# Pairing the last four token blocks already in the first half of a two-pass MLP behind a retention attention

## The chip, the cores and the metric

The kernel runs on one core of one Trainium2 chip. The metric is the time of one execution on the device in microseconds (us). Five engines work side by side, each through its own queue of instructions in order: TensorE (PE, matrix products), VectorE (DVE), ScalarE (ACT), GpSimd (POOL) and SyncE (SP, which here issues every DMA).

## The reference, cut to what matters

```python
B, H, S, D = 8, 8, 576, 64                       # attention
scores = q @ k.T / sqrt(D)                       # for each batch and head
ret    = scores * Dmat                           # gamma**(i-j) for i >= j, else 0
x      = (ret @ v) -> (B*S, H*D) = (4608, 512)   # heads side by side
h      = x @ w_in                                # 512 -> 2048
g      = max(h, 0) + alpha * min(h, 0)
out    = g @ w_out                               # 2048 -> 512
```

All inputs and the output are float32.

## The kernel before, in words

**Attention.** Eight batches times four pairs of heads make 32 joints, the first eight (two batches) worked in parts at the start. Of a joint, `operands` scales and transposes q and k; `joint` computes the values of the joint before it (`values`, L851) and its own scores and chunk sums on PE (L903, L910, L913), masks the scores on DVE (L931), sums the chunks on ACT and DVE in `su` (L943 to L954), and DMAs `su` into `vn`, from where the next call's values read it. ACT copies the values into the block's x tile (`keep_x`, L870). Values go to the PSUM banks `psh`, scores and sums to `psa`. `todo` says after which cell a joint is called.

**The MLP.** 4608 tokens are 18 blocks of 256 (`kb`). 2048 hidden columns are eight units `u` of 256. Weights of four units fit in SBUF (`wsl`), so there are two halves: all blocks with units 0 to 3, then all with 4 to 7. What a block has summed in the first half goes to DRAM (`ok`) and comes back (`op`) in the second; a block's x goes to DRAM (`xk`) and back too. `order` lists the visits (a block and its units), and a cell is one unit of one visit.

Every float32 operand is written as three pieces of which a product takes three matmuls. `split_x` makes those of a block's x, `split_w` those of a weight matrix, `split_g` (L1204 to L1211, two steps on ACT and two on POOL) those of the activated hidden block `g`. Some of the DVE and POOL steps are chained by `lock=True`: one that follows on the other engine waits for the one before.

A cell's first layer is `unit` for one block: 24 matmuls of 256 columns (L1151), 12 for each half of the unit's hidden columns, and for each half ACT, DVE, ACT, DVE (L1158 to L1165) into `ga`. `unit_two` does it for two blocks at once: 2 x 12 matmuls of 512 columns (L1181), the halves in `psh` and `psa`, the same four steps at twice the width (L1187 to L1193). The second layer, `second`, is 12 matmuls of 512 columns for a cell (L1232) into four banks `pso`; after a visit's last cell `evacuate` (L1250 to L1255) writes the sum out.

Before the change the first half is 17 blocks one by one and then block 17 with all eight units in one visit; the second half is 16 blocks in 8 pairs, and the last one single. Pairs may use `psa` since attention has ended by then (its last call stands after cell 56; the first 68 cells are the first half). In pairs, x pieces lie in turn in the room that unit 3's weights leave and in the two rooms `lxs` (`two_rooms`). The weights of unit 4 lie in twelve `planes`, the tiles that attention has left (`kx`, `qx`, `kn`, `kT`, `qT`, `at`, `su`, `wa`); those of units 5 to 7 take the rooms of units 0 to 2. Their 16 matrices come back from DRAM and are split while single blocks still run (`late`).

**What sets the order.** All steps are recorded with a cost, then `plan` puts them in an order engine by engine, by due times worked out backwards; PE may take any of the next 150 recorded steps. On the chip each engine follows that order strictly. `LAG` and `PUMP` say how many second layers stay behind the first ones. 

## Time and profile before

| | us |
|---|---|
| median of 3 runs | 931.44 |
| lowest and highest | 930.61, 931.87 |
| profiled execution, its own time | 930.41 |
| its span in the profile | 928.7 |

Busy time of the engines in the profiled execution: PE 918.4 us, weight loads 779.4, DVE 532.5, ACT 552.6, POOL 579.3. The costliest groups of PE are L1232 (second layer), L1151 (first layer of single blocks) and L1181 (of pairs). The matmuls are pipelined, so that the mean duration of one (392 ns with 512 columns, 284 with 256) is longer than the time from one to the next; what a group takes of PE's time is read from the chain of work. A few per cent of the matmuls have no record in the trace, so the counts that matter are taken from the built order of instructions.

### The profile page before, as it was taken

The page shows a single profiled execution, that of the slowest core. Times are in us where ns is not written, and L with a number is a line of the kernel's source. Part 1 is how long each engine was busy: PE and PEld are TensorE (multiplying, and loading weights), DVE is VectorE, ACT ScalarE, POOL GpSimd, SP SyncE. Part 2 cuts the span into 40 slices and gives each one's busy share as a digit, 9 for nine tenths or more (in the row PEclk, how much of TensorE's full clock was granted, in tenths as well). Part 3 has the DMA queues.
Part 4 walks back from the last instruction along what each step waited for, and adds up shares of the span by engine and source line. Part 5 has one row for each costly group of instructions (what it writes and reads, how often), then busy time and mean ns, then how long its engine had stood idle before and what let it go on. Part 6 is the DMA issues. An engine that isn't in the chain of part 4 may idle for free.

```text
span 928.7 us, 20968 instructions
## 1 busy us (share of the span) xinstructions
PE 918.4 (99%) x8101; PEld 779.4 (84%) x8101; DVE 532.5 (57%) x1070; ACT 552.6 (60%) x1178; POOL 579.3 (62%) x491
## 2 busy tenths in 40 slices
PE   8999999999999999999999999999999999999998
PEld 7676798988888898988999988888888888888887
DVE  7677666667666667766755764443454444434333
ACT  4566557566666667666876885554546363635342
POOL 5676867558765677655666465837465655647363
PEclk9999999999999999999999999999999999999999
DMA  9997587798887859864444421121212222221112
GB/s 231 241 233 144 127 203 151 176 206 175 195 199 193 193 138 221 191 150 130 148 137 147 126 80 68 47 91 46 91 54 82 68 86 95 70 68 46 46 46 68
DMA packets 235524, 120.93 MB, mean 130 GB/s; under 512 B 203408, under 2 KB 203424, under 8 KB 235424
## 3 DMA queue, kind: packets, MB, share of 16 engines
q1 hardware_dynamic: 235424, 119.59, 50.9%
q8 instruction: 64, 1.05, 0.5%
q14 instruction: 36, 0.29, 0.1%
HBM read 74.19 MB, written 31.98 MB: 114 GB/s over the span
## 4 chain that ended last, share of the span: by engine, by line
PE 90%; DMA 3%; DVE 2%; POOL 2%; SPq 1%; issue 1%; ACT 1%; POOLq 0%; DVEq 0%; ACTq 0%
PE pso L1232 39%; PE psh L1151 22%; PE psh L1181 9%; PE psa L1181 9%; PE psh L851 3%; PE psa L913 2%; PE psh L1082 2%; PE pso L1113 1%; SPq L208 1%; POOL w L775 1%; DMA kn<-in_k_dram 1%; DMA w<-in_moe_w_in_dram 1%; PE psh L903 1%; PE psa L910 1%; DMA lx<-in_moe_w_in_dram 0%
## 5 line engine op out<-in xcount | busy, mean ns | idle before, releaser
L1232 PE MATMUL pso<-w,g 128*128 128x512 f32 x1416 | 347.1, 392 | 0.0
L1232 PEld LDWEIGHTS pso<-w,g 128*128 128x128 f32 x1416 | 259.6, 188 | 50.7
L1151 PEld LDWEIGHTS psh<-lx,w 128*128 128x128 f32 x1608 | 202.4, 191 | 8.4 <-ACT x L870 1.1
L1151 PE MATMUL psh<-lx,w 128*128 128x256 f32 x1608 | 208.5, 284 | 0.7 <-ACT x L870 0.5
L1211 POOL TENSOR_TENSOR g<-g 128x512 fp32r<-128x512 f32 x136 | 176.0, 1294 | 24.2 <-DVE w L1057 4.1
L1208 POOL TENSOR_TENSOR g<-ga,g 128x512 fp32r<-128x512 f32 x72 | 93.2, 1294 | 122.9 <-ACT g L1204 107.9
L1159 DVE SCALAR_TENSOR_TENSOR ga<-psh,ga 128x256 f32<-128x256 f32 x144 | 60.6, 421 | 70.6 <-ACT ga L1158 68.9
L1158 ACT COPY ga<-psh 128x256 f32<-128x256 f32 x144 | 53.5, 372 | 69.5 <-PE psh L1151 60.8
L1208 POOL TENSOR_TENSOR g<-x,g 128x512 fp32r<-128x512 f32 x40 | 51.7, 1295 | 63.5 <-ACT g L1204 61.0
L1165 DVE SCALAR_TENSOR_TENSOR ga<-psh,malpha,ga 128x256 f32<-128x256 f32 x144 | 68.6, 477 | 22.4 <-ACT psh L1162 21.4
L1061 POOL TENSOR_TENSOR lx<-lx 128x512 fp32r<-128x512 f32 x48 | 61.9, 1296 | 20.1 <-DVE lx L1057 13.1
L1162 ACT ACTIVATE psh<-ga 128x256 f32<-128x256 f32 x144 | 55.7, 387 | 30.4 <-DVE ga L1159 30.2
L1204 ACT ACTIVATE g<-ga 128x512 fp32r<-128x512 f32 x72 | 45.4, 631 | 22.3 <-DVE ga L1165 15.0
L1208 POOL TENSOR_TENSOR g<-vn,g 128x512 fp32r<-128x512 f32 x24 | 31.1, 1294 | 41.6 <-ACT g L1204 38.4
L931 DVE SCALAR_TENSOR_TENSOR at<-psa,pf,mask 64x512 f32<-64x512 f32 x48 | 36.0, 750 | 25.8 <-PE psa L910 24.9
L1206 ACT ACTIVATE g<-ga 128x512 fp32r<-128x512 f32 x72 | 44.7, 621 | 0.0
L1250 DVE TENSOR_TENSOR op<-pso,op 128x512 f32<-128x512 f32 x34 | 23.3, 686 | 36.8 <-PE pso L1232 36.7
L1204 ACT ACTIVATE g<-x 128x512 fp32r<-128x512 f32 x40 | 25.1, 630 | 32.1 <-PE pso L1232 17.1
L1188 DVE SCALAR_TENSOR_TENSOR x<-psh,x 128x512 f32<-128x512 f32 x20 | 13.8, 690 | 45.0 <-PE psh L1181 45.0
L851 PEld LDWEIGHTS psh<-at,vn 128*64 128x64 f32 x864 | 27.7, 137 | 10.8 <-issue 6.0
L1057 POOL TENSOR_TENSOR lx<-x,lx 128x512 fp32r<-128x512 f32 x24 | 31.1, 1295 | 8.7 <-ACT lx L1054 5.4
L1181 PE MATMUL psh<-lx,w 128*128 128x512 f32 x144 | 34.7, 389 | 0.0
(292 smaller groups left out, 1695.9 us busy)
## 6 DMA issues: line engine op xcount, KB each, us to landing
xk<-x SPq DMA_DIRECT2D x18, 512.0 KB, 4.1
out_dram<-o SPq DMA_DIRECT2D x36, 256.0 KB, 2.0
ok<-o SPq DMA_DIRECT2D x34, 256.0 KB, 3.2
x<-xk SPq DMA_DIRECT2D x17, 512.0 KB, 5.7
op<-ok SPq DMA_DIRECT2D x17, 512.0 KB, 4.0
qx<-in_q_dram SPq DMA_DIRECT2D x96, 72.0 KB, 3.4
kx<-in_k_dram SPq DMA_DIRECT2D x96, 72.0 KB, 3.1
kn<-in_k_dram SPq DMA_DIRECT2D x48, 144.0 KB, 3.7
```

The costliest lines, as they stand in the source:

```text
L851: nc.tensor.matmul(pv[i].get()[half(h2), (j - js[0]) * C:(j - js[0] + 1) * C], vns[n % 2][:, h2, j], mt.get()[:, h2, j], start=True, stop= ...
L1061: lambda l=l, d=d, h=view(0, c): nc.gpsimd.tensor_tensor(out=piece(d()), in0=h(), in1=l(), op=ALU.subtract),
L1151: nc.tensor.matmul(at(b), w[:, c0:c0 + P], xp(l, cc), start=(n == 0 and cc == 0), stop=(n > 0 and cc == NCC - 1), skip_group_check=True)
L1158: do("ACT", 0.36, lambda g=g, at=at: nc.scalar.copy(g(), at(1)), [(ph, 1)], [(ga, f)])
L1159: do("DVE", 0.42, lambda g=g, at=at: nc.vector.scalar_tensor_tensor(out=g(), in0=at(0), scalar=ONE, in1=g(), op0=ALU.mult, op1=ALU.subtrac ...
L1162: do("ACT", 0.39, lambda g=g, at=at: nc.scalar.activation(at(1), g(), ACTF.Relu, scale=-1.0), [(ga, f)], [(ph, 1)])
L1165: do("DVE", 0.48, lambda g=g, at=at, fc=fc: nc.vector.scalar_tensor_tensor(out=g(), in0=at(1), scalar=malpha[:, fc:fc + 1], in1=g(), op0=A ...
L1181: nc.tensor.matmul(p.get(), w[:, c0:c0 + P], piece(words_of(g)[:, o:o + DM]), start=(l != 1 and cc == 0), stop=(l > 0 and cc == NCC - 1))
L1204: do("ACT", 0.64, lambda: nc.scalar.mul(piece(to.get()[:, 2]), whole(), BELOW), both, [(to, 2)])
L1208: do("POOL", 1.29, lambda: nc.gpsimd.tensor_tensor(out=piece(to.get()[:, 1]), in0=whole(), in1=to.get()[:, 2], op=ALU.subtract), both + [( ...
L1211: do("POOL", 1.29, lambda: nc.gpsimd.tensor_tensor(out=piece(to.get()[:, 2]), in0=to.get()[:, 0], in1=to.get()[:, 1], op=ALU.subtract), [( ...
L1232: nc.tensor.matmul(a[2 * m + b].get(), piece(g.get()[:, l, f, m * P:(m + 1) * P]), w_piece(u, 2 + f, l), start=(cell["first"] and f == 0 a ...
```

## The change

- The order of visits. Blocks 0 to 15 with units 0 to 3, then blocks 16 and 17 with units 3, 0, 1, 2; then the second half, which begins with blocks 16 and 17 and goes on with 0 to 15.
- Blocks 0 to 13 of the first half stay single; blocks 14 and 15, and 16 and 17, make two pairs, and all 18 blocks of the second half make nine. The second half's first pair reads the x pieces that the first half's last pair has made.
- The x pieces of the first pair (14, 15) lie in the twelve planes; those of the second in `lxs`.
- The 16 late weight matrices are split in pairs 1 and 2 (counted from 0), their raw words in the `ga` tiles of single blocks, with the ACT, POOL and DVE steps that the first 16 matrices have always had; the form through PSUM goes, as does that of `split_x`.
- Attention is called after other cells: its last values after cell 53, in the visit of block 13.
- The 16 conversions of second-half weights begin at cell 8 instead of 10.

```diff
@@ tile_retnet_parallel__then__act_prelu_kernel
+    PAIRS_AT = [8, 10, 12, 14, 16, 18, 20, 22, 24, 26, 29, 31, 33, 35, 37, 39, 42, 44, 46, 48, 49, 50, 51, 53]
@@ split_w
         do("ACT", 0.64, lambda: nc.scalar.mul(h(), full(), BELOW), [key], [w[0]])
-        if raw:
-            hp = Gen(psa[at % 2])
-            do("ACT", 0.6, lambda: nc.scalar.mul(piece(hp.get()), full(), BELOW), [key], [(hp, 0)])
-            do("DVE", 0.69, lambda: nc.vector.tensor_tensor(
-                out=l(), in0=full(), in1=hp.get(), op=ALU.subtract), [key, (hp, 0)], [w[1]])
-            do("DVE", 0.69, lambda: nc.vector.scalar_tensor_tensor(
-                out=d(), in0=hp.get(), scalar=ONE, in1=full(), op0=ALU.mult,
-                op1=ALU.subtract), [key, (hp, 0)], [w[2]])
-            return
         do("POOL", 1.29, lambda: nc.gpsimd.tensor_tensor(
             out=l(), in0=full(), in1=hf(), op=ALU.subtract), [key, w[0]], [w[1]], lock=True)
         do("DVE", 0.7, lambda: nc.vector.scalar_tensor_tensor(
@@ order
-    order = [(kb, (0, 1, 2, 3)) for kb in range(NKB - 1)]
-    order += [(NKB - 1, range(NU))]
-    order += [(kb, (4, 5, 6, 7)) for kb in range(NKB - 1)]
+    order = [(kb, (0, 1, 2, 3)) for kb in range(NKB - 2)]
+    order += [(kb, (3, 0, 1, 2)) for kb in (NKB - 2, NKB - 1)]
+    order += [(kb, (4, 5, 6, 7)) for kb in (NKB - 2, NKB - 1, *range(NKB - 2))]
@@ two_rooms
     def two_rooms(n):
-        if n % 2:
+        if n == 0:
+            rooms_of = ((g, i * DM) for g, i in planes())
+            return {(l, cc): next(rooms_of) for l in range(3) for cc in range(NCC)}, DM
+        if n == 1 or n % 2 == 0:
             gg = [Gen(x) for x in lxs]
             return {(l, cc): (gg[cc // 2], (l * 2 + cc % 2) * DM)
                     for l in range(3) for cc in range(NCC)}, DM
@@ split_x
-        late = vis["n"] >= LATE_X and rooms is None
...
-                if late:
-                    h = Gen(psa[n])
-                    ht = lambda h=h: h.get().rearrange("p (c t) -> p c t", t=TB)
-                    do("ACT", 0.6, lambda c=c, ht=ht: nc.scalar.mul(piece(ht()), raw(c), BELOW),
-                       keys, [(h, 0)])
-                    do("DVE", 0.7, lambda c=c, ht=ht, l=l: nc.vector.tensor_tensor(
-                        out=piece(l()), in0=raw(c), in1=ht(), op=ALU.subtract),
-                        keys + [(h, 0)], key(1, c))
-                else:
-                    do("ACT", 0.64 if wide else 0.38,
-                       lambda c=c, d=d: nc.scalar.mul(piece(d()), raw(c), BELOW), keys, key(2, c))
-                    eng, cost, tt = (("POOL", 1.29, nc.gpsimd) if rooms is None else
-                                     ("DVE", 0.69 if wide else 0.42, nc.vector))
-                    do(eng, cost, lambda c=c, l=l, d=d, tt=tt: tt.tensor_tensor(
-                        out=piece(l()), in0=raw(c), in1=d(), op=ALU.subtract),
-                        keys + key(2, c), key(1, c), lock=True)
+                do("ACT", 0.64 if wide else 0.38,
+                   lambda c=c, d=d: nc.scalar.mul(piece(d()), raw(c), BELOW), keys, key(2, c))
+                eng, cost, tt = (("POOL", 1.29, nc.gpsimd) if rooms is None else
+                                 ("DVE", 0.69 if wide else 0.42, nc.vector))
+                do(eng, cost, lambda c=c, l=l, d=d, tt=tt: tt.tensor_tensor(
+                    out=piece(l()), in0=raw(c), in1=d(), op=ALU.subtract),
+                    keys + key(2, c), key(1, c), lock=True)
@@ after the start
-    for i, at in enumerate((8, 10, 12, 14, 16, 18, 20, 22, 24, 26, 29, 31, 33, 35, 37, 39, 42, 44, 46, 48, 50, 52, 54, 56)):
+    for i, at in enumerate(PAIRS_AT):
...
-    turn = cells.index(next(c for c in cells if c["u"] == NS)) - NS
-    late = {turn - 8 + 2 * i: [16 + i] for i in range(4)}
-    for i in range(3):
-        for n in range(4):
-            late.setdefault(turn + 1 + i + n // 2 * LAG, []).append(20 + 4 * i + n)
...
-    ahead = {10 + 3 * i: 1 for i in range(16)}
+    ahead = {8 + 3 * i: 1 for i in range(16)}
@@ start_x, two
     def start_x(vis):
         kb = vis["kb"]
-        if "from" not in vis and (kb not in xb or NPAIR * (ready_kb[kb] + 1) in done):
+        if vis.get("two", (0,))[0] == 2:
+            at, step, side = visits[vis["n"] - 2]["x"]
+            vis["x"] = at, step, side
+        elif "from" not in vis and (kb not in xb or NPAIR * (ready_kb[kb] + 1) in done):
             fetch_x(vis)
-    turned_to = next(v["n"] for v in visits if 4 in v["us"])
-    two = [(visits[n], visits[n + 1]) for n in range(turned_to + 1, len(visits) - 1, 2)]
+    singles = NKB - 4
+    two = [(visits[n], visits[n + 1]) for n in range(singles, len(visits), 2)]
     for i, (va, vb) in enumerate(two):
         va["two"], vb["two"] = (i, 0), (i, 1)
-    visits[-1]["two"] = len(two), 0
@@ at_cell and after
-        for at in late.get(n, ()):
-            if at == 16:
-                planes_of.append(planes())
-            split_w(at, raw_room(), [next(planes_of[0]) for _ in range(3)] if at < 20 else None)
...
+    def split_first(at):
+        if not planes_of:
+            planes_of.append(planes())
+        split_w(at, Gen(gas[at % 2]), [next(planes_of[0]) for _ in range(3)])
...
     for cell in cells[8:]:
         vis = cell["vis"]
-        if vis["n"] > turned_to:
+        if vis["n"] == singles:
             break
         at_cell(cell)
         nxt = vis["n"] + 1
-        if vis["n"] < turned_to:
-            if cell["last"] or vis["n"] > 3:
-                start_x(visits[nxt])
-                if cell["last"]:
-                    next_x(visits[nxt])
-        elif cell["u"] in (NS + 1, NS + 2):
-            next_x(visits[nxt + cell["u"] - NS - 1])
-
-    ga_rooms = [xs[2], xs[3], xs[4]]
-    ga_kept = [raw_rooms[n] for n in range(2)]
-    nga = [0]
+        if nxt == singles:
+            if cell["u"] > 1:
+                next_x(visits[nxt + cell["u"] - 2])
+        elif cell["last"] or vis["n"] > 3:
+            start_x(visits[nxt])
+            if cell["last"]:
+                next_x(visits[nxt])
+
+    ga_rooms = [xs[3], xs[4], xs[2]]
+    nga = [3]
@@ pump
         for _ in range(k):
             if queue and "ga" in queue[0]:
                 ahead_g(1)
-                second(queue.pop(0))
+                c = queue.pop(0)
+                second(c)
+                if c["vis"]["n"] == singles + 3 and c["u"] < NS - 1:
+                    split_later(c["u"], 1)
                 ahead_g()
+
+
+    def split_later(u, half_of):
+        for n in range(2):
+            at = (NS + 1 + u) * 4 + 2 * half_of + n
+            split_w(at, Gen(gas[at % 2]))
@@ the loop over pairs
+            if i == 1:
+                if nu < 2:
+                    split_first(16 + 2 * nu)
+                    split_first(17 + 2 * nu)
+                if a["u"] < NS - 1:
+                    split_later(a["u"], 0)
             nxt = va["n"] + 2 + (nu - 1)
             if nu in (1, 2) and nxt < len(visits):
                 next_x(visits[nxt])
-    for cell in of[visits[-1]["n"]]:
-        unit(cell)
-        queue.append(cell)
-        pump(3)
-        ahead_g()
```

In the lines above `two_rooms` counts pairs from 0, `NS` is 4, `NKB` 18 and `NU` 8.

More of the change, by code (lines that the diff above doesn't have):

```diff
@@ L1260, in evacuate @@
             P * DM * 4, [(o, 0)], [(okm[kb], m)])
-    LATE_X = next(v["n"] for v in visits if 4 in v["us"]) - 3
     spare = Gen(lxs[1])
@@ L1401 @@
     todo = {}
-    for i, at in enumerate((8, 10, 12, 14, 16, 18, 20, 22, 24, 26, 29, 31, 33, 35, 37, 39, 42, 44, 46, 48, 50, 52, 54, 56)):
+    for i, at in enumerate(PAIRS_AT):
         todo.setdefault(at, []).append(2 * NPAIR + 1 + i)
     assert sum(map(len, todo.values())) == len(pairs) - 2 * NPAIR
-    turn = cells.index(next(c for c in cells if c["u"] == NS)) - NS
-    late = {turn - 8 + 2 * i: [16 + i] for i in range(4)}
-    for i in range(3):
-        for n in range(4):
-            late.setdefault(turn + 1 + i + n // 2 * LAG, []).append(20 + 4 * i + n)
-    raw_rooms = [Gen(None) for _ in range(2)]
-    ahead = {10 + 3 * i: 1 for i in range(16)}
-    nraw = [0]
-    def raw_room():
-        n = nraw[0] % 3
-        nraw[0] += 1
-        if n == 2:
-            return Gen(xs[3])
-        g = Gen(None)
-        was = raw_rooms[n] if raw_rooms[n].ops else vnm[n]
-        g.before, g.tile = list(was.ops), vns[n]
-        raw_rooms[n] = g
-        return g
+    of = {}
+    for cell in cells:
+        of.setdefault(cell["vis"]["n"], []).append(cell)
+    raw_rooms = [Gen(None) for _ in range(2)]
+    ahead = {8 + 3 * i: 1 for i in range(16)}
     def planes():
@@ L1477 @@
     planes_of = []
-    of = {}
-    for cell in cells:
-        of.setdefault(cell["vis"]["n"], []).append(cell)
+    def split_first(at):
+        if not planes_of:
+            planes_of.append(planes())
+        split_w(at, Gen(gas[at % 2]), [next(planes_of[0]) for _ in range(3)])
     for cell in cells[8:]:
         vis = cell["vis"]
-        if vis["n"] > turned_to:
+        if vis["n"] == singles:
             break
@@ L1504, in ga_room @@
         g = Gen(None)
-        g.before, g.tile = list(ga_kept[n - 3].ops), vns[n - 3]
-        ga_kept[n - 3] = g
+        g.before, g.tile = list(raw_rooms[n - 3].ops or vnm[n - 3].ops), vns[n - 3]
+        raw_rooms[n - 3] = g
         return g
```

## The prediction

> **What bounds the kernel.** I read the busy shares first, then who TensorE (PE) waits for, then the chain that ended last.
>
> ```profile
> span 928.7 us, 20968 instructions
> PE 918.4 (99%) x8101; PEld 779.4 (84%) x8101; DVE 532.5 (57%) x1070; ACT 552.6 (60%) x1178; POOL 579.3 (62%) x491
> PE 90%; DMA 3%; DVE 2%; POOL 2%; SPq 1%; issue 1%; ACT 1%; POOLq 0%; DVEq 0%; ACTq 0%
> ```
>
> PE is busy throughout and makes 90% of the chain. The view of stretches says where it is not:
>
> ```profile
> 0.00:60.00 60.00, 54.42 (x921) 40.53 (x921) 42.26 (x104) 31.27 (x53) 36.88 (x47) 1.00 1.00 241
> 60.00:440.00 380.00, 378.93 (x4764) 327.76 (x4766) 258.29 (x567) 244.73 (x580) 256.72 (x206) 1.00 0.78 176
> 440.00:548.00 108.00, 108.00 (x720) 98.36 (x715) 68.89 (x141) 83.93 (x188) 65.84 (x56) 1.00 0.43 137
> 548.00:888.00 340.00, 340.00 (x1499) 280.56 (x1498) 148.14 (x232) 178.22 (x329) 197.63 (x167) 1.00 0.20 66
> ```
>
> Columns: stretch, length, busy PE, weight loads, DVE, ACT, POOL, clock, DMA share, GB/s. PE is idle 5.6 us in the start, 1.1 us during attention (60 to 440), nothing after. So removed PE work comes off the end one for one, and each new PE wait goes on it one for one.
>
> The price of the two forms stands in the chain, single blocks first, then pairs (start, us, what, how many matmuls):
>
> ```profile
> 486.49 2.87 PE psh L1151 x24
> 489.37 2.75 PE pso L1232 x12
> ...
> 627.33 2.72 PE psh L1181 x12
> 630.05 2.72 PE pso L1232 x12
> 632.77 2.72 PE psa L1181 x12
> ```
>
> 24 matmuls of 256 columns take 2.87 us (119.6 ns each); 12 of 512 take 2.72 (226.7 ns), or 2.75 where 256-column ones follow.
>
> **What the Trainium skill says.** "Perfetto Trace Analysis", Identifying the Most-Contended Engine: matmul busy share is a bad measure of headroom, the weight-load share a better one. That is 84% here, so PE idles little but is not at its peak. "TensorE: Matmul & The Clock Gate", Back-to-back issue gap: an isolated gap of N/2.4 + 2.5 ns, as an estimate 109 and 216 ns; the trace has 120 and 227. The same section's sustained 131 ns at N = 512 does not hold in this trace. Doubling N thus saves little: 12.5 ns a pair. "SBUF — State Buffer", Two separate sides: DVE and GpSimd share a port pair under an exclusive lock. The trace agrees in kind: DVE waited 19.2 us in 7 waits for POOL before L1057.
>
> **The change, part by part.**
>
> 1. *Wider first matmuls.* The built instruction order has 1728 matmuls of L1151 before and 1152 after, 768 of L1181 before and 1056 after, L1232 1632 in both. Blocks 14 to 17 in the first half are 8 pair-units; in the second half two blocks that ran single become 4 more. Each of the 12 saves 2 x 2.87 - 2 x 2.72 = 0.30 us: 3.6 us. Their 24 second-layer batches go from 2.75 to 2.72: 0.7 us. **Sum: -4.3 us**, all on the path.
>
> 2. *Pieces and transfers.* Block 16 is split once, not twice, one x read of 512 KB goes, one output round trip (512 KB each way) comes with 2 + 2 DVE evacuation steps of 0.69 us. All lies beside PE, in stretches with DMA at 0.2 to 0.43 and DVE at 44 to 64%. I take 0; without that cover the late piece would be op, at L1250, and so the pso banks.
>
> 3. *Second-half weights.* 16 matrices are split during pairs 1 and 2. Each loses an ACT and a DVE step (0.60 and 0.68 us), and its L775 form (1.28 us, POOL) with L777 (0.69 us, DVE) replaces the PSUM form. A pair-unit lasts 10.88 us on PE; POOL's four steps of L1208 and L1211 fill 5.2. The 16 need 16 x (1.28 + 0.69) = 32 us of the shared lock, about 6 units of slack; they stand over some 7, and pair 2 splits no x. Two raw rooms of gas, each held for a landing (3.0 us, as vn<-wk) and 2.6 us of steps, pass 16 in 45 of those 76 us. Hidden: 0. If not, g is late and L1232 waits: 0 to 3 us.
>
> 4. *Attention ends three cells earlier* (56 to 53), joints 28 to 32 at cells 48 to 53. From a joint's scores to its values runs a chain: scores, ACT and DVE sums into su, two DMAs vn<-su, values. For the joint whose scores end at 413.09:
>
> ```profile
> 418.01 1.15 SPq L208 DMA_DIRECT2D vn<-su  x2
> ```
>
> Issue after 4.9 us; what is written to su and vn around it lands in
>
> ```profile
> DMA to landing us min/median/max: 2.5/3.3/4.0
> ```
>
> and the second of the two landed 8.0 us after the scores. Joining scores, issues and landings over 24 joints gives 6.7 to 12.2, median 9.1. Now PE's cover, from the built order priced as above: joints 26, 28, 29, 30, 31 had 11.1, 11.2, 11.2, 9.9, 14.0 us and get 8.9, 8.2, 8.8, 9.6, 8.5. Before, PE never came sooner than 9.2. In the new order the sums of joints 28 to 30 stand early on DVE and ACT; adding up what stands before them puts the issue near 3.5 and the landing near 7.8: no wait. Joint 31 is different: DVE has, between scores and the steps that free psh for the last values, 2 masks of 0.75, 2 of 0.28, L945 0.48, three L951 (0.83), L954 0.41, a weight's 0.42 + 0.42 + 0.69, two evacuations of 0.69, four L1159 (0.42), three L1165 (0.48): 9.8 us, plus 0.2 of hand-over, against 8.5 on PE. **Wait: 1.5 us.** It stops everything behind it on PE: cells 54 and 55, both with their operands there. Joint 30's scores wait for a last L1165 (0.35), a unit of cell 53 for psh (0.15).
>
> 5. *Pieces of blocks 14 and 15 move into the attention buffers.* The third piece lies in at, su and wa, so it starts after the last values: 8 DVE steps of 0.42 and 8 POOL steps of 0.74, alternating under the lock, 9.3 us with the first held until ACT and POOL finish cell 53's g. PE's cover is 6 + 24 + 12 + 24 + 6 matmuls: 1.37 + 2.87 + 2.75 + 2.87 + 1.37 = 11.2 us. I take 0.1 us for cell 55, which waits for a psh that DVE frees between such steps. Bounds 0 to 3 (one POOL step of g, 1.29, slipping in twice).
>
> Waits 1.5 + 0.35 + 0.15 + 0.1 = 2.1; net 2.1 - 4.3 = **-2.2 us**. The start is reordered in small ways: 0, bounds -0.5 to +0.5. The profiled execution took 930.41 (span 928.7 and 1.7 around it), so 928.2 against itself; the median shown is 931.44, 1.0 above it, so **929.2**.
>
> **The rivals.**
>
> *All of it arrives.* The DVE queue ahead of the last values drains early because ACT feeds it sooner, no wait: 931.44 - 4.3 = 927.1. For it: joint 9 had 8.5 us of cover already and cost about 0.5. Against it: 9.8 us of DVE work in 8.5.
>
> *A wash.* The landing stays at the median of before, 9.1, also where PE is close: joint 26 waits 0.2, 28 0.9, 29 0.3, and with the 2.1 that makes 3.5: 930.6. For it: the median. Against: those joints were in no hurry.
>
> *Slower.* One mechanism: the chain scores, su, DMA, values in the five tight joints. With landing time L their waits are 5L - 44.0, plus 0.6 from the rest of parts 4 and 5. It passes the saving at L = 9.5 and makes the kernel slower by over 0.2% from L = 9.9. At 10.2, which joint 29 took before, waits are 7.6: 934.7. For it: joints now come every 8.7 to 12 us instead of 13.7, and SyncE spends some 10 us issuing for one. Against: after joint 29 no q or k loads remain.
>
> *It doesn't do what it says:* excluded by the counts of step 1.
>
> **How the numbers follow.** 0.2% is 1.9 us, about what a measurement of this kernel can tell from no change. Likeliest case 0.45, its own range 928.2 to 930.0, mostly below 929.6; all arrives 0.15; wash 0.27; slower 0.13. Faster: 0.15 + 0.40 = 0.55. Same: 0.27 + 0.05 = 0.32. Slower 0.13. The range goes from just below full arrival, 926.9, to 932.0, past the wash; most of the slower case and the luckiest start stay out.
>
> **What would show it.** In the changed kernel, 24 matmuls of the new pairs' form at 2.72 per 12; no PE wait in the pairs, which would confirm step 3; a PE wait of 1 to 2 us ahead of the last values, released by DVE and not by a DMA; the first pair starting without a gap (step 5). Waits released by vn<-su at several joints mean the wash or worse; a POOL-released wait of L1232 in pairs 1 and 2 proves step 3 wrong. A time under 926 or over 935 would mean that I missed a mechanism.

## Result and the profile after

The changed kernel took **934.0 us** in the median of 22 runs (931.1 to 937.9), the kernel before 931.9 beside it (22 runs, 930.0 to 934.3). The ratio is 1.0024, 95% interval 1.0015 to 1.0033. The forecast was 929.2 with 926.9 to 932.0: the kernel came out 2.1 us slower instead of 2.2 faster. It lost 4.3 us more than was forecast.

The profiled execution took 935.48 us, 1.5 above the median; that of before, at 930.41, lies 1.5 under its own. So the two traces differ by 5.1 us where the medians differ by 2.1. The page of the changed kernel, busy line and chain:

```profile
span 933.8 us, 20314 instructions
PE 918.5 (98%) x7813; PEld 767.2 (82%) x7813; DVE 518.1 (55%) x1010; ACT 537.2 (58%) x1116; POOL 596.0 (64%) x507
PE 77%; POOL 8%; DMA 5%; SPq 3%; issue 3%; ACT 2%; DVE 1%; POOLq 0%; ACTq 0%; DVEq 0%
```

PE has 288 matmuls fewer and is just as long busy. Its share of the chain fell from 90 to 77%, that of POOL and DMA together rose from 5 to 13. The stretches of the changed kernel (same columns as in the prediction):

```profile
60.00:140.00 80.00, 77.34 (x1019) 58.28 (x1019) 55.19 (x110) 49.57 (x108) 56.11 (x47) 0.98 0.74 164
140.00:340.00 200.00, 199.03 (x2483) 177.30 (x2478) 140.54 (x314) 134.30 (x323) 141.06 (x113) 1.00 0.85 198
340.00:442.00 102.00, 100.02 (x1258) 88.29 (x1257) 68.32 (x154) 66.18 (x166) 59.52 (x50) 1.00 0.77 185
442.00:888.00 446.00, 445.75 (x1967) 367.60 (x1966) 196.43 (x306) 241.53 (x445) 282.08 (x237) 1.00 0.23 74
```

and of the kernel before:

```profile
60.00:140.00 80.00, 79.41 (x1119) 61.57 (x1120) 55.80 (x112) 48.79 (x110) 57.94 (x48) 1.00 0.78 162
340.00:442.00 102.00, 101.94 (x1282) 90.40 (x1281) 67.81 (x155) 65.10 (x160) 64.65 (x51) 1.00 0.68 163
```

PE is idle 2.66 us from 60 to 140 (0.59 before) and 1.98 from 340 to 442 (0.06). After 442 it is idle 0.25 in 446. PE's waits say for what:

```profile
PE psh L843 <- DMA vn<-su: 1.8, 3, 1.3
PE psh L843 <- DVE ga L1150: 1.2, 1, 1.2
PE psh L1136 <- DVE ga L1150: 0.9, 2, 0.6
PE psa L905 <- DMA vn<-in_v_dram: 0.5, 1, 0.5
PE pso L1217 <- POOL g L1196: 0.3, 1, 0.3
```

L843 are attention's values, L905 its scores and states, L1136 a single block's first matmuls, L1217 the second layer. L1150 is the step that frees psh. The first line is the largest; 1.6 of its 1.8 us stand at joint 9 (near 123 us), where nothing was forecast. The second is the wait ahead of the last values, forecast at 1.5.

**A measure that idle time does not give.** Idle time does not hold all that a wait costs. Joint 9 shows it (start, duration, idle before):

```profile
120.32 1.55 PE L1217 MATMUL pso<-w,g 128*128 128x512 f32 x6
121.80 0.34 PE L843 MATMUL psh<-at,vn 128*64 128x64 f32 x4
123.41 0.33 PE L843 MATMUL psh<-at,vn 128*64 128x64 f32 x2 [1.27 <-DMA vn<-su]
124.06 1.87 PE L843 MATMUL psh<-at,vn 128*64 128x64 f32 x30 [0.32 <-DMA vn<-su]
125.86 0.37 PE L895 MATMUL psh<-qT,kT 64*64 64x64 f32 x2
```

36 values take 1.20 us where nothing waits. Here 4.06 us pass from the first to the scores behind them: 2.86 lost, of which 1.59 is idle. Of the other 1.27, 0.8 is lost by the last 30 values, during which the clock stood at half (last section); for some 0.5 the trace shows the first values as long and not as late. In the second profile of this kernel (experiment 1), at full clock, 2.44 are lost here and 1.9 are idle. So I compare kernels by PE's **loss**: the time from one start to the next, less the price of the instructions between (119.6 ns a matmul of 256 columns, 226.7 of 512, 1.20 us for 36 values, 1.26 for 68 of scores). The matmuls of the three MLP lines are all in these traces (1728, 768 and 1632 before, 1152, 1056 and 1632 after), so none of these losses is a missing record. By stages, in us, one profiled execution each (after_x3c20 is left out here and told of in its place):

| kernel | time over before, 95% | 100–140 | 140–340 | 340–450 | 450–end |
|---|---|---|---|---|---|
| before | – | 1.3 | 5.5 | 2.6 | 1.5 |
| changed, first profile | 1.0024 (1.0015–1.0033) | 3.8 | 6.3 | 5.5 | 1.4 |
| changed, second profile | 1.0025 (1.0015–1.0036) | 2.5 | 7.6 | 5.6 | 1.4 |
| after_split: the changed kernel's order, its first matmuls in 12 pair-units narrower | 1.0056 (1.0034–1.0077) | 2.2 | 6.8 | 4.6 | 1.7 |
| before_tight | 1.0025 (1.0016–1.0034) | 1.6 | 6.8 | 5.7 | 1.3 |
| before_start | 1.0026 (1.0015–1.0037) | 1.8 | 6.3 | 6.0 | 1.5 |
| before_ahead8 | 0.9997 (0.9984–1.0010) | 1.3 | 5.4 | 3.0 | 1.6 |
| before_conv60 | 0.9993 (0.9981–1.0004) | 2.3 | 5.2 | 2.7 | 1.4 |
| before_su15p | 1.0047 (1.0029–1.0065) | 2.2 | 8.6 | 5.5 | 1.4 |
| after_even | 1.0034 (1.0020–1.0048) | 2.8 | 10.6 | 4.3 | 0.7 |
| after_even_su15 | 1.0048 (1.0030–1.0065) | 2.3 | 11.0 | 4.9 | 1.0 |
| after_hold | 1.0034 (1.0021–1.0046) | 1.1 | 8.3 | 4.9 | 0.9 |
| after_x3 | 1.0012 (1.0004–1.0021) | 1.5 | 6.5 | 5.3 | 4.8 |
| after_x3t1 | 1.0029 (1.0017–1.0041) | 2.0 | 6.5 | 4.2 | 4.6 |
| after_x3t2 | 0.9983 (0.9971–0.9996) | 1.6 | 6.7 | 2.9 | 2.4 |
| after_x3t2c45 | 1.0019 (1.0004–1.0035) | 2.6 | 7.0 | 6.2 | 0.7 |
| after_x3t3c20 | 0.9969 (0.9958–0.9980) | 1.6 | 10.0 | 3.1 | 0.9 |

The names are those of the experiments below. The difference between the two traces then adds up: +1.0 in the first 52 us, where both kernels have the same order on PE (chance); +1.6 from there to the scores of joint 8 (experiment 1 shows how much executions differ there); +2.5, +0.8, +2.9 and -0.1 in the four stages; -3.6 for 12 pair-units at 0.30. That is +5.1. (The 0.7 for second-layer batches at 2.72 instead of 2.75 lies in the losses.)

### The profile page after: what moved, and what is told of

The parts are those of the page before. It is cut to its first block, busy times and chain, and to the rows that moved or that the text cites. A ratio compares the mean times of both kernels' runs of the same rounds, so it can differ in the third digit from the quotient of the medians.

```text
span 933.8 us, 20314 instructions
## 1 busy us (share of the span) xinstructions
PE 918.5 (98%) x7813; PEld 767.2 (82%) x7813; DVE 518.1 (55%) x1010; ACT 537.2 (58%) x1116; POOL 596.0 (64%) x507
## 4 chain that ended last, share of the span: by engine, by line
PE 77%; POOL 8%; DMA 5%; SPq 3%; issue 3%; ACT 2%; DVE 1%; POOLq 0%; ACTq 0%; DVEq 0%
PE pso L1217 34%; PE psh L1136 12%; PE psa L1166 12%; PE psh L1166 11%; SPq L208 3%; PE psh L843 3%; POOL g L1196 2%; POOL g L1193 2%; PE psa L905 2%; PE pso L1098 1%; DMA w<-in_moe_w_in_dram 1%; POOL w L767 1%; DMA vn<-su 1%; PE psh L1067 1%; POOL lx L1046 1%
## 5 line engine op out<-in xcount | busy, mean ns | idle before, releaser
L1217 PE MATMUL pso<-w,g 128*128 128x512 f32 x1416 | 345.3, 391 | 0.3 <-POOL g L1196 0.3
L1217 PEld LDWEIGHTS pso<-w,g 128*128 128x128 f32 x1416 | 261.0, 188 | 52.8 <-POOL g L1196 1.0
L1136 PE MATMUL psh<-lx,w 128*128 128x256 f32 x1152 | 150.8, 285 | 0.9 <-DVE ga L1150 0.9
L1136 PEld LDWEIGHTS psh<-lx,w 128*128 128x128 f32 x1152 | 144.7, 190 | 7.8 <-DVE ga L1150 2.5
L1193 POOL TENSOR_TENSOR g<-ga,g 128x512 fp32r<-128x512 f32 x48 | 61.9, 1290 | 82.4 <-ACT g L1189 44.6
L1143 ACT COPY ga<-psh 128x256 f32<-128x256 f32 x96 | 35.6, 371 | 39.6 <-PE psh L1136 36.6
L1144 DVE SCALAR_TENSOR_TENSOR ga<-psh,ga 128x256 f32<-128x256 f32 x96 | 40.4, 421 | 28.0 <-ACT ga L1143 26.5
L1150 DVE SCALAR_TENSOR_TENSOR ga<-psh,malpha,ga 128x256 f32<-128x256 f32 x96 | 45.7, 479 | 17.0 <-ACT psh L1147 16.6
L1166 PE MATMUL psh<-lx,w 128*128 128x512 f32 x228 | 54.8, 389 | 0.0
L1166 PE MATMUL psa<-lx,w 128*128 128x512 f32 x228 | 54.8, 389 | 0.0
L1166 PEld LDWEIGHTS psa<-lx,w 128*128 128x128 f32 x228 | 42.8, 188 | 8.9
L1147 ACT ACTIVATE psh<-ga 128x256 f32<-128x256 f32 x96 | 37.1, 387 | 19.6 <-DVE ga L1144 19.4
L1189 ACT ACTIVATE g<-ga 128x512 fp32r<-128x512 f32 x48 | 30.3, 630 | 20.1 <-DVE ga L1150 10.1
```

What stands on the lines that cost most here:

```text
L1136: nc.tensor.matmul(at(b), w[:, c0:c0 + P], xp(l, cc), start=(n == 0 and cc == 0), stop=(n > 0 and cc == NCC - 1), skip_group_check=True)
L1143: do("ACT", 0.36, lambda g=g, at=at: nc.scalar.copy(g(), at(1)), [(ph, 1)], [(ga, f)])
L1144: do("DVE", 0.42, lambda g=g, at=at: nc.vector.scalar_tensor_tensor(out=g(), in0=at(0), scalar=ONE, in1=g(), op0=ALU.mult, op1=ALU.subtrac ...
L1147: do("ACT", 0.39, lambda g=g, at=at: nc.scalar.activation(at(1), g(), ACTF.Relu, scale=-1.0), [(ga, f)], [(ph, 1)])
L1150: do("DVE", 0.48, lambda g=g, at=at, fc=fc: nc.vector.scalar_tensor_tensor(out=g(), in0=at(1), scalar=malpha[:, fc:fc + 1], in1=g(), op0=A ...
L1166: nc.tensor.matmul(p.get(), w[:, c0:c0 + P], piece(words_of(g)[:, o:o + DM]), start=(l != 1 and cc == 0), stop=(l > 0 and cc == NCC - 1))
```

## The experiments

### 1. The same kernel again

> The changed kernel once more, for a second profile beside the other three on one chip. Three losses are in question, as its first profile shows them: the start (scores of joint 8 at 99.6 us instead of 97.0), joint 9 (its values wait 1.6 us for vn<-su, then the clock is near 0.55 for 2 to 3 us, 2.6 in all), and the joints from 26 on (about 3). If they are effects of the new order, they recur here within 1 us each: scores of joint 8 at 98.5 to 100.5, joint 11 at 139 to 141, first pair near 444. If the start's loss is only the timing of one execution, joint 8 comes at 96.5 to 98 here. Median expected 933 to 935.

Measured: 935.0 against 932.7 for before on that chip. Joint 8's scores came at 98.1, joint 11's at 137.8, the first pair near 443. So joint 9's wait recurs (2.4 us lost), and the end's (5.6). The start is another matter. From the scores of part 3 of the start (52 us) to those of joint 8 it took 46.1 us here and 46.9 in the first profile. Six profiled kernels in which these operations stand exactly as in before took 45.0 to 47.4, on average 45.9. Three later runs have the new start too: before_start (47.6), after_split (47.9) and after_hold (47.6). The five executions of it take 47.2 on average. So the new start costs about 1.3 us, while single executions of one order differ by up to 2.4.

### 2. The close end alone, the start's order alone, the conversions' places alone

before_tight is the kernel before with this line changed:

```
-    for i, at in enumerate((8, 10, ... 46, 48, 50, 52, 54, 56)):
+    for i, at in enumerate((8, 10, ... 46, 48, 49, 50, 51, 53)):
```

> The kernel before, with only attention's last joints moved to cells 48, 49, 50, 51, 53 (instead of 48, 50, 52, 54, 56); the order up to 172 us is that of before. Theory of the tight end: the waits that the changed kernel shows between joint 28 and the last values (by its profile about 3 us) come here too: 934 to 936. Theory of the conversions (and of the start): only the wait ahead of the last values, 1.2, and small ones: 932 to 933.5.

Measured: 935.9 against 932.7, ratio 1.0025. From 340 to 450 it loses 5.7 us, about as the changed kernel does (5.5 and 5.6, in after_split 4.6), where before loses 2.6. **The close end, with the order that the planner makes for it, costs 3 us there, with neither pairs nor moved conversions beside it.** Its waits from 140 us on:

```profile
PE psh L851 <- DMA vn<-su: 1.5, 3, 0.7
PE psh L851 <- DVE ga L1165: 0.4, 1, 0.4
```

0.7 of the first line and all of the second stand after 340 us; in the changed kernel DVE makes the largest wait there. What is the closeness and what the new order, this run cannot part: before_start, next, loses as much in that stretch with its joints where they were.

before_start gives the first 474 operations of before the due times that the planner gave them in the changed kernel (START is that list):

```
         last = -min(due)
+        for n, t in enumerate(START):
+            due[n] = t / 1e3 - last
```

> The kernel before, with the first 474 operations (to about 100 us) given the due times that the planner gave them in the changed kernel, so that they come in the changed kernel's order: first difference at 44 us on SP and 58 us on PE. Theory of the start: joint 8's scores come 2 to 3 us later than 97.0, the whole 933 to 935. Theory that the start's loss is the timing of one execution: 931 to 932.5, joint 8 within 1 us of 97.0.

Measured: 935.8, ratio 1.0026; joint 8's scores at 99.4. The stretch from part 3's scores to joint 8 takes 47.6 us, just above the highest of the order of before. Half of the loss is elsewhere: from 340 to 450, where no due time was touched, it loses 6.0 instead of 2.6. The planner is one greedy pass. Another start leaves other engines free at other times, and every later choice is made anew. So **a new order alone**, with the same work, brings 3 us of waits to places that the edit did not touch.

before_ahead8 has the conversions created at the changed kernel's cells:

```
-    ahead = {10 + 3 * i: 1 for i in range(16)}
+    ahead = {8 + 3 * i: 1 for i in range(16)}
```

> The kernel before, with the sixteen conversions of second-half matrices at cells 8, 11, ... 53 as in the changed kernel, instead of 10, 13, ... 55; the order up to 107 us is that of before. Theory of the conversions: the first one's load, store and its steps on ACT, POOL and DVE stand in joint 9's chain; its vn<-su are issued 1 us later, land near 10.8 instead of 9.1 us after the scores, the values wait 1 to 2 us, the clock drops behind that wait: joint 11's scores 1.5 to 3 us later than in before (135.2), the whole 933 to 935. Theory of the tight end: the conversions cost nothing, 931 to 932.5.

Measured: 932.8 against 932.7, no difference. But the run did not do what it was meant for. The stores wk<-wa, one for each conversion, start at 211 us in before and at 211 here: the planner goes by due times and not by the cell at which a conversion is created. In the changed kernel the first store is at 116 us and the last at 432; in before 211 and 492. Experiment 5 asks why.

### 3. The wide matmuls undone

```
-  nc.tensor.matmul(p.get(), w[:, c0:c0 + P], piece(words_of(g)[:, o:o + DM]), ...)
+  for s in (((0, DM),) if va["two"][0] not in (0, 1, 10) else ((0, TB), (TB, DM))):
+      nc.tensor.matmul(p.get()[:, s[0]:s[1]], w[:, c0:c0 + P],
+                       piece(words_of(g)[:, o + s[0]:o + s[1]]), ...)
```

> The changed kernel in the changed kernel's order, with the first matmuls of 12 pair-units (the pairs 0, 1 and 10) each issued as two of 256 columns: 24 in 2.87 us instead of 12 in 2.72. Theory that the wide matmuls bring what the prediction counted: each of the 12 pair-units takes 0.30 us longer, 3.6 in all, so 2.5 to 4.7 us over the changed kernel's median (2.3 over before's in the first two measurements), 5 to 7 over before's. Rival, that the saving is lost in the pairs because something else sets their pace: at most 1.5 over the changed kernel.

Measured: ratio 1.0056 (1.0034 to 1.0077) against the changed kernel's 1.0025, so 0.31%, 2.9 us; 3.6 was worked out, and the interval holds it. Its chain in the first pair:

```profile
445.42 2.88 PE psh L1167 x24
...
452.86 2.87 PE psh L1167 x24
```

In the changed kernel the same batches stand as forecast:

```profile
444.40 2.72 PE psa L1166 x12
447.12 2.72 PE psh L1166 x12
```

The saving is real and it arrives. The rival that pairs lose it is out.

### 4. Even joints, and a longer landing in the planner

after_even spreads the joints, after_even_su15 also tells the planner of later landings, before_su15p does only that, on the kernel before with its start held by a START list:

```
-    PAIRS_AT = [8, 10, ... 24, 26, 29, 31, ... 46, 48, 49, 50, 51, 53]
+    PAIRS_AT = [8 + 2 * i for i in range(23)] + [53]
```

```
-            return 2.0 if d.late else ...
+            return 2.0 + d.more if d.late else ...
...
             dma(to, lambda h2=h2: su.get()[half(h2)], (S - C) * D * 4, keys, [(vn, "s", h2)])
+            ops[-1].more = 1.5
```

> The changed kernel with attention's joints spread evenly: cells 8, 10, 12, ... 52 and 53, instead of a close end at 48, 49, 50, 51, 53. The planner then gives the first 100 us almost the order of before (the same on PE). PE's work between scores and values, from the built order: 9.9 us and more for the joints 9 and 26 to 30 (8.5 to 9.6 in the changed kernel), 7.1 for the last. If the close end and the start's order are the losses, 3 to 5 us go: 929.5 to 932 on the scale where before has 932.7, 0.5 to 3 faster than before. If spreading only moves the waits to other joints: 933.5 to 936, no better than the changed kernel.

> The kernel of the evenly spread joints, and in the planner 1.5 us more for the two transfers vn<-su (it assumes 2.5 us from issue to landing, the profile of before showed 3.3 in the median and up to 4.0). PE's work between scores and values in the built order is then 9.5 us or more for every joint from 9 on (11.1 for joint 9). Theory of late landings: the waits for vn<-su are gone, loss over the ideal price of PE's instructions after 100 us as in before (11 us) or less, 928 to 930.5 where before has 932.7. Rival, that DVE's and POOL's queues set the waits and not the landings: no better than the evenly spread kernel, 931 or more.

> The kernel before, with only the planner's 1.5 us more for vn<-su, and the start's order held as in before. Joint 9 gets 9.9 us of PE work instead of 8.5, nearly all others 9.8 or more as they had already. If the planner's short landing costs before anything, it is the waits of joint 9 and those near 295 us, about 1 us: 931 to 932.5 where before has 932.7. A gain of 2 us or more would say that the edit by itself, and not the spread joints, makes the gain of its neighbour.

Measured: 935.9, 937.8 and 937.7 against 933.2. None helped; the kernel before lost 4.4 us by the planner's edit alone. The theory of late landings falls: among after_even's PE waits from 100 to 450 us none is for vn<-su, and yet it loses 10.6 us from 140 to 340. What took their place (after_even, from 100 us):

```profile
PE pso L1217 <- DVE o L1240: 1.5, 1, 1.5
PE psh L1136 <- DVE ga L1150: 1.3, 2, 0.7
PE pso L1217 <- POOL g L1196: 1.1, 2, 0.8
```

DVE's order around the largest of them (start, duration, idle before):

```profile
204.71 0.78 DVE L821 STREAM_TRANSPOSE kT<-kx 128x576 f32<-128x576 f32 x1 [1.91 <-DMA vn<-su]
205.72 0.47 DVE L1150 SCALAR_TENSOR_TENSOR ga<-psh,malpha,ga 128x256 f32<-128x256 f32 x1
206.10 0.68 DVE L1240 SCALAR_TENSOR_TENSOR o<-pso,o 128x512 f32<-128x512 f32 x1
```

A transpose of the next joint's keys stands at the head of DVE's queue and waits 1.9 us for a transfer (the trace names vn<-su as the last), and behind it stand the steps that free psh and pso for PE. From 100 to 340 us DVE is busy 166 of 240 us, 69% of the time. Here it is the queue's head that costs.

### 5. The buffer behind the conversions

In the changed kernel wa becomes the last of the planes for the pieces of blocks 14 and 15. So it must be free when the first pair is prepared, and wa is also the tile through which all 16 conversions of second-half matrices go. Followed back from the end, this makes all 16 due earlier; in the traces the first store starts at 116 us and not at 211. after_x3 takes another tile, so that the results `ga` of the pairs go round four tiles and not five:

```
-            rooms_of = ((g, i * DM) for g, i in planes())
+            rooms_of = ((g, i * DM) for g, i in planes(xs[3]))
...
-    def planes():
+    def planes(last=was):
...
-        for x in (sus, was):
+        for x in (sus, last):
...
-    ga_rooms = [xs[3], xs[4], xs[2]]
+    ga_rooms = [xs[4], xs[2]]
```

before_conv60 leaves the kernel before as it is and makes the conversions due 60 us earlier. after_hold is the changed kernel with the first conversion held until 136 us. after_x3c20 is after_x3 with conversions due 20 us earlier and created at the cells of before. The edit of the due times (60 or 20) and that of the hold:

```
+        due = [t - op.soon for t, op in zip(due, ops)]
...
+            first = len(ops)
             convert((op_, 0), was, None)
+            for op in ops[first:]:
+                op.soon = 60
```

```
+            for op in ops[first:] if n == min(ahead) else ():
+                op.hold = 136
```

> The changed kernel with one plane of the first pair's pieces moved out of wa, into the ring tile x3 (the eight ga rooms of the pairs then go round four tiles instead of five). In the changed kernel wa must be free at cell 54, so the 16 conversions of second-half matrices, which use wa, run from 116 us (first store wk) to 432 us, all beside attention; in before they ran from 211 to 492. With wa left alone the planner puts them back to about 200 to 497 and PE's order is that of before up to 107 us. Theory of the conversions: the start, joint 9 and the joints up to 25 lose what they lose in before; PE's loss over the ideal price between 100 and 340 us falls from 10 to about 7 us, the start is 1 us shorter; left are the pairs' saving of 4.3 and the close end's 2.5 to 3: 1 to 2.5 us below before. Rival, that any new order of the joints loses this much: 1 to 4 us above before, as in the changed kernel.

> The kernel before, with only the conversions' due times 60 us earlier in the planner: they then run from about 150 to 445 us, nearly all beside attention, as in the changed kernel, and not from 211 to 492. Blocks, joints and pairs are those of before. Theory of the conversions: their four DVE and POOL steps and their loads and stores stand in the joints' chains and ahead of the steps that free psh; 2 to 4 us slower than before. Rival, that the conversions hide wherever they stand: within 1 us of before.

> The changed kernel, with only the first conversion held back in the planner until 136 us, so that its two loads, its steps on ACT, DVE and POOL and its store no longer stand in the start's end and in joint 9's chain; PE's order is the changed kernel's up to 130 us. If that conversion makes joint 9's wait: PE's loss over the ideal price between 100 and 140 us falls from 2.3 to 3.8 (three executions) to 1.3 to 1.8, and the median comes 1 to 2 us under the changed kernel's, 0 to 1.5 over before. If joint 9 waits because its values stand earlier in PE's order (8.6 us after the scores instead of 9.2, and in one piece): 2.3 or more stays.

> The kernel with the plane in x3 and the changed kernel's close end, with the conversions at 10, 13, ... 55 and their due times 20 us earlier: they end near 480 instead of 497 in the planner (505 in the execution of the kernel with the plane in x3). There the pairs lost 4.8 us after 450 (1.4 in before and in the changed kernel), in three waits for POOL's g at 448, 559 and 573. If those came from late conversions and the weights behind them: 1.5 to 2.5 after 450, and 2 to 3 us under that kernel, 0.5 to 2 under before. If from the ga rooms, four instead of five: 4 or more stays.

Measured: after_x3 934.1 against 933.1, ratio 1.0012, half the changed kernel's excess. From 100 to 140 us it loses 1.5, as before does: joint 9's wait is gone. But now waits stand in the pairs, where the conversions end at 505 us. Its waits from 440 us on:

```profile
PE pso L1217 <- POOL g L1196: 2.2, 3, 0.8
```

4.8 us are lost there, against 1.4. So it did not come out 1 to 2.5 us below before, as the theory of the conversions had it; at 0.9 us above, it lies just under the 1 to 4 us that the text gave to its rival, any new order.

before_conv60 came out at 932.5 against 933.1: early conversions alone cost nothing (stores from 147 to 441 us). So it is not their number beside attention that costs. What differs in the changed kernel is that the first comes already in joint 9's chain. SyncE's queue there, changed kernel:

```profile
115.89 0.57 SPq L208 DMA_DIRECT2D wk<-wa  x1
116.51 1.98 SPq L208 DMA_DIRECT2D qx<-in_q_dram  x3
118.59 1.29 SPq L208 DMA_DIRECT2D kn<-in_k_dram  x2
119.99 1.21 SPq L208 DMA_DIRECT2D vn<-su  x2
```

and before, for the same joint:

```profile
115.41 0.57 SPq L208 DMA_DIRECT2D ok<-o  x1
116.09 1.14 SPq L208 DMA_DIRECT2D vn<-su  x2
```

DVE's last sum (L946; L954 in before) ends at 117.4 in the changed kernel and at 115.1 in before. From there to its issue vn<-su waits 2.6 us in SyncE's queue, 1.0 in before: a store of the conversion and the reads moved behind it stand ahead. It is issued 6.8 us after the scores (5.5 in before) and lands at 10.8 (9.1), while PE comes for the values at 8.6 (9.2).

after_hold took that conversion away. From 100 to 140 it loses 1.1: the wait is gone, as that theory has it. Joint 9's values lose 2.86, 2.44 and 1.91 us in the three executions of the changed order (the third is after_split) and 0.19 here; in the other runs it is at most 0.6, but 1.56 in after_x3t2c45 (experiment 6), whose first store comes at 143 us. An early conversion does not always bring the wait: after_even, with a first store at 120 us, loses nothing at these values. But the kernel took 936.0 against 932.9, and the loss from 140 to 340 rose to 8.3. The largest of its waits from 100 us on is

```profile
PE psh L895 <- DVE ga L1150: 3.0, 3, 1.5
```

4 us are lost at 133, 154, 163 and 176 us. At the largest of these waits DVE's queue has the same head as in after_even, a transpose of keys that waits for its load, ahead of the steps L1150 that free psh:

```profile
164.95 0.78 DVE L821 STREAM_TRANSPOSE kT<-kx 128x576 f32<-128x576 f32 x1 [2.69 <-DMA kx<-in_k_dram]
```

The conversions are packed closer there (stores at 147, 162, 179 and 193 us; 116, 150, 173 and 187 in the changed kernel); that this makes the load late was not shown.

after_x3c20: 935.2 against 932.9. The conversions ended at 498, not at 480. After 450 it lost 2.7 (4.8 in after_x3), where I had expected 1.5 to 2.5. With the kernels of experiment 6 the loss after 450 goes with the start of the last conversion's store: 4.8 at 505 us, 4.6 at 503, 2.4 at 501, 2.7 at 498, 0.9 at 490, 0.7 at 463. That points to late conversions and the weights behind them, but these were not followed one by one. The fewer `ga` tiles alone are not it: the kernel with 0.9 has four as well. Nor is it all: a wait for POOL's g of 0.95 stands in the first pair both in after_x3 (at 450 us) and in the kernel whose conversions end at 463 (at 449, so that the table has it under 340–450). The profile of after_x3c20, at 941.1, lies 6 us above its median, with 3.6 and 4.6 us lost at two joints that wait for su; I draw nothing else from it.

### 6. Versions with another end

All four leave wa alone and create the conversions at 10, 13, ... 55. The last eight joints, in place of 42, 44, 46, 48, 49, 50, 51, 53:

```
 after_x3t1     41, 44, 45, 47, 49, 50, 51, 53
 after_x3t2     41, 42, 45, 46, 48, 50, 51, 53
 after_x3t2c45  the same, conversions due 45 us earlier
 after_x3t3c20  41, 42, 44, 46, 48, 50, 52, 53, conversions due 20 us earlier
```

> As the kernel with the plane in x3, and the last eight joints at cells 41, 44, 45, 47, 49, 50, 51, 53 instead of 42, 44, 46, 48, 49, 50, 51, 53, the conversions at 10, 13, ... 55 as in before; PE's order is that of before up to 249 us. If the close end's 2.5 to 3 us come from five joints within six cells, spreading it over 13 cells takes 1 to 2 of them: 2.5 to 4 us below before. If each new order brings its own small waits: no better than the kernel with the plane in x3 alone.

> As its neighbour, with the last eight joints at 41, 42, 45, 46, 48, 50, 51, 53; PE's order is that of before up to 174 us. Same expectations: 2.5 to 4 us below before if the spread end helps, no better than the kernel with the plane in x3 alone if each order brings its own waits.

> As its neighbour, with the last eight joints at 41, 42, 44, 46, 48, 50, 52, 53, so that no three stand in consecutive cells. Between 340 and 450 the close end lost 5.3 to 5.7 us, before 2.6, and the one spread end that is measured (41, 42, 45, 46, 48, 50, 51, 53) 2.9. If the spacing decides: 2.5 to 3.5 there, 3 to 5 us under before in all. If that 2.9 was luck of one order: 4 or more there, 0 to 2 under before.

> The kernel that came out 1.6 us under before (plane in x3, last joints at 41, 42, 45, 46, 48, 50, 51, 53), with the conversions' due times 45 us earlier. It lost 2.4 after 450 with conversions until 501; with them done near 460 that should be 1.4. The first conversions then stand near 133 us, and joint 10 and 11 may lose for it: 1.5 to 3.5 between 100 and 140 instead of 1.6. Both together: within 1.5 us of that kernel.

Measured, against 933.1 for the first two and 932.9 for the others: 935.4, 931.6, 930.2 and 934.1 (in the order of the texts above). The ends with no three joints in neighbouring cells lose 2.9 and 3.1 from 340 to 450, like before's 2.6; x3t1, with 49, 50, 51, loses 4.2. But x3t2c45 has x3t2's end and loses 6.2 (5.3 without the pair's wait at 449), and before_start and before_su15p, with the end of before, lose 6.0 and 5.5. No kernel with three joints in neighbouring cells lost under 4.2 there, so in these runs the spacing is needed, and it is not enough.

**after_x3t3c20 beats both kernels**: 930.2 us in the median of 22 runs, ratio to before 0.9969 (0.9958 to 0.9980). Its page is from its slowest execution (933.42 us, span 931.7); the busy line:

```profile
PE 915.7 (98%) x7813; PEld 764.1 (82%) x7813; DVE 517.6 (56%) x1010; ACT 536.9 (58%) x1116; POOL 595.9 (64%) x507
```

It came out of several orders that were tried. Part of its lead over before may be luck of this one order, as part of before's lead over others seems to be.

## Why the prediction was wrong

*Step 1, the saving: right.* New pairs at 2.72 for 12, and undoing them costs it again (experiment 3). A reading beside it was wrong: DVE's waits for POOL before L1057 (19.2 us in 7) do not show the port lock of the hardware. The program itself lets each step with `lock=True` wait for the one before it on the other engine, and no run here shows more than that. Step 3's 32 us follow from that chain and stand.

*Steps 2 and 3, pieces and second-half weights hidden: right in the second half.* PE waits 0.3 us there, once: at 570 us, in pair 2, for POOL's g. That is the sign that the text named against step 3, at a size that does not matter. But the cover had a price that step 3 did not look for. With wa left alone (after_x3), so that the conversions are not forced into attention, just the wait that step 3 named, L1217 behind POOL's g, came, with 3.4 us more loss in the pairs.

*Step 4, the close end: right in kind, mis-sized.* Forecast 2.0: 1.5 ahead of the last values, 0.35 at joint 30's scores, 0.15 for a unit. In losses it was 1.36 ahead of the last values, 1.08 at joint 30's scores (L1150, and a late v load that nothing had priced), and 0.36 and 0.56 at the values of joints 28 and 29, for which the text had no wait. Together 3.4, and the stage's excess over before is 2.9. The term that was mis-sized is the landing of su, "near 7.8": where it could be read it was 8.7 for joint 28, 10.6 for joint 29 and 8.4 for joint 31. The slower rival, five joints at one landing time, is not what happened either: su held up two values, DVE the last ones, a v load one joint's scores.

*Step 5, the plane in wa: the step whose mechanism failed.* It said that the third piece lies in at, su and wa, and asked only when they come free for the pieces. For the pieces it was right: the first pair starts at 444.40 without a gap. It did not ask who else uses wa. That is the 16 conversions, which it moved from 211–492 to 116–432 us. Step 4 counted the DVE steps of one conversion ahead of the last values; that all 16 move was priced nowhere, so at nothing. Here 16 x 6 steps on ACT, DVE and POOL with their loads and stores were moved by 60 to 112 us. Their direct cost is joint 9's wait: from 100 to 140 us 0.9 to 2.5 us more loss than in before in three executions, gone in after_x3 and after_hold, which take that conversion away from it. Taking it away did not make the whole faster by as much: after_x3 came out 1 us nearer to before, after_hold no nearer.

*"The start is reordered in small ways: 0, bounds -0.5 to +0.5": too narrow.* It took 0.8 and 1.6 us more than in before's profile, and some 1.3 on average over five executions (experiment 1). What the term left out altogether is that a reordered start re-makes the order behind it. From 140 to 340 the two profiles lose 0.8 and 2.1 more than before.

The sum in the two profiles: -3.6, +0.8 to 1.6 (start), +1.2 to 2.5 (joint 9), +0.8 to 2.1 (140 to 340), +2.9 (the end), in place of -4.3 + 2.1; the medians, 2 us over before, ask for the lower values. **The expected gain went into waits ahead of the pairs**, some two fifths of them where the prediction looked and three fifths where it did not. That 934.0 lies near the 934.7 of the slower rival is chance, for the mechanism is another.

What stays open: the losses from 140 to 340 us. No run pins them to one part of the change. One thing goes with the plane in wa: DVE's idle time ahead of the transposes of q and k (L821) from 100 to 340 us is 10.1 to 13.3 us in the changed kernel's three executions and after_hold, 9.3 and 15.0 in the two kernels of even joints, 4.6 in before and 3.3 to 6.7 in all others. But PE's loss does not follow it: after_x3t3c20 loses 10.0 from 140 to 340 with 6.1 of it. In the kernel before, whose work did not change, before_su15p lost 3.1 us more there, and before_tight 1.3. The table suggests that nearly every new order has such waits: of its 14 edited orders all but before_ahead8 and before_conv60 lost more than 13 us after 100 us, where before lost 11. How much of the close end's 3 us is such a draw is open too; that before's order is in some way fitted to the chip is a guess.

## What to carry to other kernels

Before a buffer gets a second use, list all that already pass through it: the new use sets a due time for each of them, and a planner carries it back through the program. Where an order is made by a greedy planner, an edit is worth its own price plus a new draw of small waits. In the five kernels here whose work is that of before it was 0, 0, 3.1, 3.2 and 4.4 us. Forecast that term, and try several orders before judging the edit. And measure a wait from start to start against the price of the work, by stages, and not by idle time alone.

## What was not expected of the hardware

*The clock was halved behind a short wait.* Around joint 9's wait (PE, weight loads, DVE, ACT, POOL, then the granted clock, which is a mean over the stretch):

```profile
122.00:124.00 2.00, 0.47 (x6) 0.19 (x2) 0.15 (x1) 1.05 (x2) 2.00 (x2) 1.00 0.88 230
124.00:126.00 2.00, 1.94 (x34) 1.83 (x38) 1.01 (x2) 1.30 (x4) 0.96 (x2) 0.55 0.94 283
126.00:128.00 2.00, 2.00 (x69) 1.93 (x70) 0.59 (x3) 0.40 (x1) 1.62 (x2) 0.60 0.78 139
124.20:127.60 3.40, 3.40 (x94) 3.28 (x94) 1.38 (x4) 1.70 (x4) 2.33 (x2) 0.50 0.86 204
```

After about 1.6 us of idle PE (by the starts, two matmuls in 2.1 us) the clock stood at 0.50 for 3.4 us. The 68 matmuls of joint 10's scores took 2.0 us instead of 1.26. The Trainium skill, "TensorE: Matmul & The Clock Gate", Part 1, What's actually happening, speaks of half clock after an idle window of about 3.4 us, a window that runs freely; here less idle was enough, and not always: after 1.2 us of idle at 431 us, and 1.9 us at joint 9 in the second profile, it stood at 1.00. In the slow profile of after_x3c20 it was at 0.50 twice more, from 293.4 to 296.8 and from 409.4 to 416.2, behind waits with 1.9 and 3.0 us of idle. That may be one source of the changed kernel's wider runs (6.8 us from lowest to highest, 4.2 for before); it was not tested.

*Issuing transfers did not have a fixed price.* Four reads qx took SyncE 1.9 us at 108 us in before, 2.9 us at 97 us, and 4.1 us at 277 us in before_tight, shortly behind a vn<-su whose values began only 5.9 us after its issue. No run here shows why.
